# Retention products regrouped, and feed-forward steps paced anew, in a one-core retention and feed-forward kernel

## The chip, the cores and the metric

The kernel runs on one core of one Trainium2 chip. The metric is the device time of one execution in microseconds (us), lower is better. A time is a median of several executions; a ratio is the mean time of one kernel's fast runs over the mean of the other's in the same rounds, so not quite the ratio of the medians. "Faster" or "slower" is said from 2% on; smaller differences are read from the 95% intervals and from the traces. All runs quoted here are of the fast state.

Names used throughout: TensorE (PE in the profile; PEld are its weight loads), VectorE (DVE), ScalarE (ACT), GpSimd (POOL).

## The reference

```python
# retention: B=8, H=8, S=576, D=64
scores = (1/sqrt(D)) * q @ k.T
ret    = scores * Dmat            # Dmat = gamma_h ** (i - j) for i >= j, else 0
attn   = ret @ v
# bridge: (B,H,S,D) -> x of (B*S, H*D) = (4608, 512)
h   = maximum(x @ w_in, 0)        # w_in (512, 2048)
out = (h * h) @ w_out             # w_out (2048, 512)
```

## The kernel before

Retention runs in chunks of 128 tokens (the last of each batch has 64), 40 in all, with a running state `u`. The feed-forward layer runs on blocks of 512 tokens. Block 0 is done in 16 plain "steps" (4 matmuls of 128x512, which the profile counts as 8), while the weights are still being converted; every later block is 28 steps of 4 smaller matmuls (Strassen-like products). The two are interleaved on TensorE: groups of small retention products, then some steps, and so on. After the last chunk come the remaining steps and the second layer (the last 403 us of the profile), which the change does not touch.

Of a chunk the retention does: transposes of q and k (`turn`), products inside the chunk for its second half (`retain_a`), products with the state (`retain_b`), scores of the next chunk (`scores`), products inside the chunk for its first half (`retain_c`), each with 8 heads.

```python
    def retain_c(i):
        own, grow = within(i, 0)
        more = ci + 1 < NCH
        if i < N_EARLY or i >= N_CH - 2:
            # a copy of 2 elements of x: retain_c waits for retain_b through it
            nc.scalar.copy(u_sb[(2 * ci + (cs // CH)) % 3][:, 0:2, 0:1], xp[0][:, :, cs - CH:cs - CH + 1])
        ...                                    # products, 2 of x and 2 of u at a time
        if more:
            grown(i, 1)                        # state u from PSUM to SBUF, on ScalarE
        ...
            while steps and steps[0][0] <= (n - 2 if n > 4 else n - 3):
                step()                         # forced: x's room is wanted
                owed[0] -= 1
            nc.scalar.copy(xT[n]..., p...)     # x from PSUM to SBUF

    def ffn(i):                                # called three times a chunk
        if tok < TOK + R_0:
            rate = (N_W1 - 2) / R_0 if tok >= TOK else 0
        elif tok < 5 * TOK:
            rate = (3 * N_MP * NP - LAG) / (4 * TOK - TOK - R_0 + TOK)
        else:
            rate = N_MP * NP / TOK
        owed[0] += cs / 3 * rate
        while steps and owed[0] >= 1:          # may be no step at all
            owed[0] -= 1
            step()
    ...
            retain_a(i - 1);  ffn(i - 1);  convert(6)
            retain_b(i - 1)
            if i < N_CH: scores(i)
            ffn(i - 1);  convert(6)
            if i + 1 < N_CH: turn(i + 1)
            retain_c(i - 1)
            ffn(i - 1);  convert(6)
```

`convert(6)` issues the six parts in which one piece of the first layer's weights is converted: five operations on VectorE and, in their midst, a pair of activations on ScalarE; a step of block 0 needs its piece. The comments in the code are mine. The program keeps `retain_c` from running beside `retain_b`, since both add into the same PSUM from different rows of the array: a step between them does it, and where there is none, the small copy. No run here tries it without.

Of the kernel before, what the change touches and what calls it, by code (L numbers as in the profile page):

```python
# [15 lines left out]
C = 128  # L16
CH = C // 2
TOK = 512
# [22 lines left out]
def kernel(  # L41
# [33 lines left out]
    nc = tc.nc  # L75
    ctx.enter_context(tc.manual_schedule())

    B, H, S, D = q.shape
# [7 lines left out]
    N_MP = N_M // 2  # L86
    N_MQ = N_M // 2
    N_BLK = n_tok // TOK
    NP = len(PRODUCTS)
    NCH = -(-S // C)  # L90
    chunks = [(b, ci, ci * C, min(C, S - ci * C)) for b in range(B) for ci in range(NCH)]
    N_CH = len(chunks)
# [62 lines left out]
    N_W1 = N_DF  # L155
# [124 lines left out]
    def fetch_raw(count):  # L280

        for _ in range(count):
            if n_raw[0] < min(N_W1, n_made[0] + N_RAW):
                fetch_w(n_raw[0])
                n_raw[0] += 1
# [23 lines left out]
    def convert(count):  # L309
        for _ in range(count):  # L310
            f = next(w_in_steps, None)
            f and f()
# [14 lines left out]
    for half in range(2):  # L327
        at = slice(CH * half, CH * half + CH)
# [4 lines left out]
    u_sb = [only.tile([128, HP, D], F32, name=f"u_sb{j}") for j in range(3)]  # L333
# [3 lines left out]
    N_EARLY = TOK // C  # L337
# [12 lines left out]
    def rows(half, n=64):  # L350
        return slice(64 * half, 64 * half + n)
# [4 lines left out]
    xp = [None]  # L356
    clean = set()

    def clears(half, bank):

        new = (half, bank) not in clean
        clean.add((half, bank))
        return new

    def turn(i):

        cs, c0 = chunks[i][3], chunks[i][2]
        n_h = cs // CH
        p = ps_t.tile([128, 2, 512], F32, tag="t", name="t_ps").rearrange("p h (j d t) -> p h j d t", j=2, d=HP)
        for j in (1, 0):  # L370
            for hp in range(HP):
                for h in range(n_h):
                    nc.tensor.transpose(p[:, h, j, hp, :], loaded[i][j][rows(h), 2 * hp:2 * hp + 2, :],  # L373
                                        ident[rows(h), rows(h)])
        for j, name in ((1, "kT"), (0, "qT")):
            t = st[i][name] = work2.tile([128, HP, C], F32, tag=name, name=name) if j == 0 else work.tile([128, HP, C], F32, tag=name, name=name)
            to = t[:, :, :cs].rearrange("p d (h t) -> p h d t", h=n_h)
            if j:
                nc.scalar.copy(to, p[:, :n_h, j, :, :])
            else:  # L380
                nc.vector.tensor_tensor(to, p[:, :n_h, j, :, :], dq[:, :, c0:c0 + cs].rearrange("p d (h t) -> p h d t", h=n_h),
                                        op=ALU.mult)
# [31 lines left out]
    def within(i, h):  # L414

        s = st[i]
        b_, ci, c0, cs = chunks[i]
        own, grow = [], []
        for hp, e, b in HEADS:
            own.append(lambda hp=hp, e=e, b=b: nc.tensor.matmul(  # L420
                x_at(hp, b, h), lhsT=s["vs"][rows(h), 2 * hp + b, :], rhs=s["ret"][rows(h), e, hp, :],
                start=clears(b, hp // 2), stop=False, skip_group_check=True))
            grow.append(lambda hp=hp, e=e, b=b: nc.tensor.matmul(  # L423
                u_ps[0][rows(e), hp, :], lhsT=loaded[i][1][rows(1 - h), 2 * hp + e, :], rhs=s["vs"][rows(1 - h), 2 * hp + b, :],
                start=(ci == 0 and h == 1 and hp == 0), stop=(hp == HP - 1), skip_group_check=True))
        return own, grow

    def grown(i, h):
        nc.scalar.copy(u_sb[(2 * chunks[i][1] + h + 1) % 3], u_ps[0])

    def retain_a(i):

        b_, ci, c0, cs = chunks[i]
        xp[0] = ps_x.tile([128, 2, 256], F32, tag="x", name="x_ps", padded_shape=[128, 2, 512])
        clean.clear()
        if ci == 0:
            u_ps[0] = ps_u.tile([128, HP, D], F32, tag="u", name="u_ps")
        if cs < C:
            return
        own, grow = within(i, 1)  # L440
        for j in range(0, len(own), 2):
            for f in own[j:j + 2] + grow[j:j + 2]:
                f()
        grown(i, 0)

    def retain_b(i):

        s = st[i]
        b_, ci, c0, cs = chunks[i]
        for h in reversed(range(cs // CH)):  # L450
            if 2 * ci + h == 0:
                continue
            u = u_sb[(2 * ci + h) % 3]
            for hp, e, b in HEADS[0:2] + HEADS[4:6] + HEADS[2:4] + HEADS[6:8]:
                nc.tensor.matmul(x_at(hp, b, h), lhsT=u[rows(e), hp, :], rhs=s["qT"][rows(e), hp, CH * h:CH * h + CH],  # L455
                                 start=clears(b, hp // 2), stop=False, skip_group_check=True)

    def retain_c(i):

        b_, ci, c0, cs = chunks[i]  # L460
        own, grow = within(i, 0)
        more = ci + 1 < NCH
        if i < N_EARLY or i >= N_CH - 2:

            nc.scalar.copy(u_sb[(2 * ci + (cs // CH)) % 3][:, 0:2, 0:1], xp[0][:, :, cs - CH:cs - CH + 1])
        for j in range(0, len(own), 2):
            for f in own[j:j + 2] + (grow[j:j + 2] if more else []):
                f()
        if more:
            grown(i, 1)  # L470
        tok = b_ * S + c0
        at = tok
        p = xp[0][:, :, 0:256].rearrange("p a (g t) -> p a g t", g=2)
        while at < tok + cs:
            n = at // TOK

            while steps and steps[0][0] <= (n - 2 if n > 4 else n - 3):
                step()
                owed[0] -= 1
            end = min(tok + cs, (n + 1) * TOK)  # L480
            nc.scalar.copy(xT[n][:, :, at - n * TOK:end - n * TOK].rearrange("p (a g) t -> p a g t", a=2),  # L481
                           p[:, :, :, at - tok:end - tok])
            at = end
            if n_next[0] < N_BLK and (n_next[0] + 1) * TOK <= at:
                steps.extend(block_steps(n_next[0]))
                n_next[0] += 1
        st[i] = loaded[i] = None
# [137 lines left out]


    steps = []
    owed = [0.0]
    w_out_steps = w_out_parts()
    n_w2 = [0]  # L630

    def block_steps(n):
        if n == 0:
            return [(0, first_in, j) for j in range(N_W1)]
        return [(n, ffn_in, n, mp, j) for mp in range(N_MP) for j in range(NP)]

    def step():
        n, f, *args = steps.pop(0)
        f(*args)

    n_next = [0]



    R_0 = TOK * 5 // 4
    LAG = 7

    def ffn(i):

        b, ci, c0, cs = chunks[max(0, min(i, N_CH - 1))]  # L650
        tok = b * S + c0
        if tok < TOK + R_0:
            rate = (N_W1 - 2) / R_0 if tok >= TOK else 0
        elif tok < 5 * TOK:
            rate = (3 * N_MP * NP - LAG) / (4 * TOK - TOK - R_0 + TOK)
        else:
            rate = N_MP * NP / TOK
        owed[0] += cs / 3 * rate
        while steps and owed[0] >= 1:
            owed[0] -= 1  # L660
            step()

    turn(0)
    for i in range(N_CH + 1):
        if i <= N_EARLY:

            convert((0, 0, 2, 5, 5)[i])
            if i >= 1:
                retain_a(i - 1)
                retain_b(i - 1)  # L670
                retain_c(i - 1)
            convert((0, 0, 1, 1, 1)[i])
            if i == N_EARLY:
                step()
            scores(i)
            if i == N_EARLY:
                convert(6)
                step()
            turn(i + 1)
            if i == N_EARLY:  # L680
                convert(5)
        else:
            retain_a(i - 1)
            ffn(i - 1)
            convert(6)
            retain_b(i - 1)
            if i < N_CH:
                scores(i)
            ffn(i - 1)
            convert(6)  # L690
            if i + 1 < N_CH:
                turn(i + 1)
            retain_c(i - 1)
            ffn(i - 1)
            convert(6)
        if i + 3 < N_CH:
            load(i + 3)
        if i < N_EARLY:
            fetch_raw(1)
# [210 lines left out]
```

## Time and profile before

| | before |
|---|---|
| time, median of 4 runs | 1025.22 us (1019.52 to 1026.13) |
| profiled execution | span 1019.0 us |
| TensorE busy | 983.6 us (97%) |
| VectorE, ScalarE, GpSimd busy | 751.6, 184.9, 80.3 us |

TensorE is the bound; its 35.4 us of idle time and the time lost inside "busy" are all there is to win. The lines that carry this are in the prediction. One table more tells who TensorE waited for (us in total, times, longest; the seven largest rows of its matmuls). It is the table to compare with every later run:

```profile
PE t_ps L373 <- DVE ret L406: 7.8, 5, 5.4
PE t_ps L373 <- DMA k_ld<-in_k_dram: 5.9, 6, 3.2
PE x_ps L455 <- ACT u_sb L429: 3.0, 6, 0.6
PE sc_ps L399 <- DVE qT L381: 2.8, 2, 1.8
PE o_a L790 <- DMA a<-g_dram: 2.6, 1, 2.6
PE x_ps L420 <- ACT room L481: 1.9, 1, 1.9
PE x_ps L420 <- ACT u_sb L465: 1.8, 5, 0.7
```

The transposes (`t_ps`) waited 7.8 us for the masking of the scores (`ret`), because both share one PSUM tile. The last row is the small copy, which only six chunks have here. The profiled execution was among the fastest of this kernel (1020.7 us), so differences of times are read from the timed runs and the trace is used to say where they lie.

### The profile page before, as it was taken

The page shows a single profiled execution, that of the slowest core. Times are in us where ns is not written, and L with a number is a line of the kernel's source. Part 1 is how long each engine was busy: PE and PEld are TensorE (multiplying, and loading weights), DVE is VectorE, ACT ScalarE, POOL GpSimd, SP SyncE. Part 2 cuts the span into 40 slices and gives each one's busy share as a digit, 9 for nine tenths or more (in the row PEclk, how much of TensorE's full clock was granted, in tenths as well). Part 3 has the DMA queues.
Part 4 walks back from the last instruction along what each step waited for, and adds up shares of the span by engine and source line. Part 5 has one row for each costly group of instructions (what it writes and reads, how often), then busy time and mean ns, then how long its engine had stood idle before and what let it go on. Part 6 is the DMA issues. An engine that isn't in the chain of part 4 may idle for free.

```text
span 1019.0 us, 24086 instructions
## 1 busy us (share of the span) xinstructions
PE 983.6 (97%) x10376; PEld 862.1 (85%) x10376; DVE 751.6 (74%) x1418; ACT 184.9 (18%) x425; POOL 80.3 (8%) x82
## 2 busy tenths in 40 slices
PE   6789999999999999999999998999999999999998
PEld 4444488888888788888788888999999999999997
DVE  2679577666888887888886776877777677777765
ACT  2435221111312213212221000000000000000000
POOL 1100001101111011110101000000000000000000
PEclk9789999999999999999999999999999999999999
DMA  8965547737578669669537898784855747565351
GB/s 201 236 191 162 131 154 204 195 122 208 159 241 270 188 227 268 219 211 288 178 146 271 337 420 307 279 288 157 290 201 200 271 167 258 193 232 207 124 207 42
DMA packets 187658, 220.34 MB, mean 216 GB/s; under 512 B 119200, under 2 KB 137632, under 8 KB 178592
## 3 DMA queue, kind: packets, MB, share of 16 engines
q1 hardware_dynamic: 187552, 218.81, 65.8%
q8 instruction: 81, 1.33, 0.5%
q14 instruction: 25, 0.20, 0.1%
HBM read 129.39 MB, written 89.39 MB: 215 GB/s over the span
## 4 chain that ended last, share of the span: by engine, by line
PE 90%; DVE 4%; DMA 2%; SPq 2%; issue 1%; ACT 1%; DVEq 0%; ACTq 0%
PE h_b L578 17%; PE o_b L790 16%; PE h_c L578 11%; PE h_a L578 11%; PE o_c L790 11%; PE o_a L790 11%; PE h_ps L543 5%; PE x_ps L420 3%; PE t_ps L373 2%; PE x_ps L455 2%; PE sc_ps L399 1%; DMA a<-g_dram 1%; DMA k_ld<-in_k_dram 1%; PE u_ps L423 1%; SPq L142 1%
## 5 line engine op out<-in xcount | busy, mean ns | idle before, releaser
L578 PE MATMUL h_b<-room,w 128*128 128x256 f32 x736 | 178.0, 385 | 0.0
L578 PEld LDWEIGHTS h_b<-room,w 128*128 128x128 f32 x736 | 136.5, 190 | 19.9 <-DVE room L597 0.3
L790 PE MATMUL o_b<-w,room 128*128 128x128 f32 x1168 | 144.5, 275 | 0.2 <-DVE room L741 0.2
L790 PEld LDWEIGHTS o_b<-w,room 128*128 128x128 f32 x1168 | 137.2, 192 | 0.5 <-DVE room L741 0.4
L790 PE MATMUL o_c<-w,room 128*128 128x128 f32 x1008 | 123.0, 275 | 0.0
L790 PEld LDWEIGHTS o_c<-w,room 128*128 128x128 f32 x1008 | 117.7, 192 | 0.0
L578 PE MATMUL h_c<-room,w 128*128 128x256 f32 x480 | 115.9, 384 | 0.0
L578 PE MATMUL h_a<-room,w 128*128 128x256 f32 x448 | 106.9, 381 | 0.0
L578 PEld LDWEIGHTS h_c<-room,w 128*128 128x128 f32 x480 | 89.2, 190 | 12.8
L578 PEld LDWEIGHTS h_a<-room,w 128*128 128x128 f32 x448 | 84.3, 190 | 12.2 <-issue 0.5
L790 PE MATMUL o_a<-w,a 128*128 128x128 f32 x688 | 85.9, 275 | 2.6 <-DMA a<-g_dram 2.6
L790 PEld LDWEIGHTS o_a<-w,a 128*128 128x128 f32 x688 | 81.3, 192 | 2.9 <-issue 2.8
L585 DVE SCALAR_TENSOR_TENSOR room<-room 128x512 f32<-128x512 f32 x96 | 69.7, 726 | 3.3
L595 POOL TENSOR_TENSOR room<-room 128x512 f32<-128x512 f32 x32 | 35.9, 1121 | 441.8 <-ACT room L594 358.7
L801 ACT COPY r<-o_a 128x128 f32<-128x128 f32 x54 | 14.4, 266 | 276.9 <-PE o_a L790 246.3
L543 PE MATMUL h_ps<-room,w 128*128 128x512 f32 x128 | 62.7, 636 | 1.0 <-ACT room L481 1.0
L420 PEld LDWEIGHTS x_ps<-ret,v_ld 64*64 64x64 f32 x1152 | 42.4, 143 | 20.1 <-issue 13.6
L597 DVE TENSOR_TENSOR room<-h_b,room 128x512 f32<-128x512 f32 x32 | 22.1, 691 | 50.1 <-PE h_b L578 47.7
L420 PE MATMUL x_ps<-ret,v_ld 64*64 64x64 f32 x1152 | 52.6, 234 | 5.7 <-ACT room L481 1.9
L408 POOL TENSOR_TENSOR v_ld<-v_ld,dv 128x512 f32<-128x512 f32 (+1 forms) x40 | 44.2, 1108 | 90.3 <-DMA v_ld<-in_v_dram 69.7
L543 PEld LDWEIGHTS h_ps<-room,w 128*128 128x128 f32 x128 | 24.5, 201 | 28.0 <-issue 25.7
L588 ACT COPY room<-h_a 128x512 f32<-128x512 f32 x32 | 18.8, 587 | 157.4 <-PE h_a L578 157.4
(94 smaller groups left out, 1361.1 us busy)
## 6 DMA issues: line engine op xcount, KB each, us to landing
g_dram<-room SPq DMA_DIRECT2D x32, 1792.0 KB, 7.3
a<-g_dram SPq DMA_DIRECT2D x43, 1024.0 KB, 6.8
room<-g_dram SPq DMA_DIRECT2D x20, 1024.0 KB, 6.0
w<-w_dram SPq DMA_DIRECT2D x7, 1792.0 KB, 12.2
out_dram<-room SPq DMA_DIRECT2D x18, 512.0 KB, 3.3
v_ld<-in_v_dram SPq DMA_DIRECT2D x32, 256.0 KB, 3.8
w<-in_moe_w_in_dram SPq DMA_DIRECT2D x16, 512.0 KB, 5.0
w<-in_moe_w_out_dram SPq DMA_DIRECT2D x16, 512.0 KB, 3.8
```

Of the source, the lines that this page charges most:

```text
L373: nc.tensor.transpose(p[:, h, j, hp, :], loaded[i][j][rows(h), 2 * hp:2 * hp + 2, :], ident[rows(h), rows(h)])
L408: nc.gpsimd.tensor_tensor(vs[:cs], vs[:cs], dv[:cs, :, ci:ci + 1].to_broadcast([cs, H, D]), op=ALU.mult)
L420: own.append(lambda hp=hp, e=e, b=b: nc.tensor.matmul(x_at(hp, b, h), lhsT=s["vs"][rows(h), 2 * hp + b, :], rhs=s["ret"][rows(h), e, hp, : ...
L455: nc.tensor.matmul(x_at(hp, b, h), lhsT=u[rows(e), hp, :], rhs=s["qT"][rows(e), hp, CH * h:CH * h + CH], start=clears(b, hp // 2), stop=Fa ...
L543: nc.tensor.matmul(p.rearrange("p h t -> p (h t)"), lhsT=w[:, c, :], rhs=xT[0][:, c, :], start=(c == 0), stop=(c == N_DM - 1))
L578: nc.tensor.matmul(p[:, mm, :], lhsT=w[:, c, :], rhs=xs[n][right][:, c, :], start=(j in OPENS and mm == 0 and c == 0), stop=(j in CLOSES a ...
L585: nc.vector.scalar_tensor_tensor(t, t, 0.0, t, op0=ALU.max, op1=ALU.mult)
L588: nc.scalar.copy(p1, p)
L595: nc.gpsimd.tensor_tensor(g["A11"], g["A11"], g["A11"], op=ALU.mult)
L597: nc.vector.tensor_tensor(g["A22"], p, p15, op=ALU.add)
L790: nc.tensor.matmul(p, lhsT=s["lefts"][left][:, m, :], rhs=w_out[j][:, m, WO_SLOT[right], :], start=(i in OPENS and m == 0), stop=(i in CLO ...
L801: nc.scalar.copy(r[:, 0, 0:128], p)
```

## The change

Its intent is fewer goings to and fro between retention and steps (two groups per chunk, not three), at least one step between any two groups, and a line that says how many steps should be done at which token. Core of the diff, comments added, cuts marked:

```diff
     def retain_b(i):
         ...
+        # now in every chunk, at the end of the products with the state
+        nc.scalar.copy(u_sb[(2 * ci + (cs // CH)) % 3][:, 0:2, 0:1], xp[0][:, :, cs - CH:cs - CH + 1])
     def retain_c(i):
-        if i < N_EARLY or i >= N_CH - 2:
-            nc.scalar.copy(...)               # the same copy
         ...
-        if more:
-            grown(i, 1)
         ...
             nc.scalar.copy(xT[n]..., p...)
+            if more and at == tok:
+                grown(i, 1)                   # behind x's copy
-    def ffn(i): ...                           # rates, as above
+    PACE = ((4 * TOK + HALF // 4, N_W1 + 2 * N_MP * NP - 2), ...)
+    def ffn(i, half):                         # called twice a chunk
+        gone[0] += chunks[...][3] / 2
+        if steps and steps[0][0] == 0:        # block 0: a step and its conversion together
+            step(); convert(6)
+            if half and steps and steps[0][0] == 0:
+                step(); convert(6)
+            return
+        ...                                   # want = the line through PACE at this token
+        if steps:
+            step()                            # never none while steps are left
+        while steps and done[0] < int(want):
+            step()
...
-            retain_a(i - 1);  ffn(i - 1);  convert(6)
-            retain_b(i - 1)
-            if i < N_CH: scores(i)
-            ffn(i - 1);  convert(6)
-            if i + 1 < N_CH: turn(i + 1)
-            retain_c(i - 1)
-            ffn(i - 1);  convert(6)
+            retain_a(i - 1)
+            if i < N_CH: turn(i)
+            ffn(i - 1, 0)
+            retain_b(i - 1)
+            if i < N_CH: scores(i)
+            retain_c(i - 1)
+            ffn(i - 1, 1)
```

More of the change, by code (lines that the diff above doesn't have):

```diff
@@ L462, in retain_c @@
         more = ci + 1 < NCH
-        if i < N_EARLY or i >= N_CH - 2:
-            nc.scalar.copy(u_sb[(2 * ci + (cs // CH)) % 3][:, 0:2, 0:1], xp[0][:, :, cs - CH:cs - CH + 1])
         for j in range(0, len(own), 2):
@@ L478, in retain_c @@
                 step()
-                owed[0] -= 1
             end = min(tok + cs, (n + 1) * TOK)
@@ L627 @@
     steps = []
-    owed = [0.0]
     w_out_steps = w_out_parts()
@@ L638, in step @@
         n, f, *args = steps.pop(0)
+        done[0] += 1
         f(*args)
     n_next = [0]
-    R_0 = TOK * 5 // 4
-    LAG = 7
-    def ffn(i):
-        b, ci, c0, cs = chunks[max(0, min(i, N_CH - 1))]
-        tok = b * S + c0
-        if tok < TOK + R_0:
-            rate = (N_W1 - 2) / R_0 if tok >= TOK else 0
-        elif tok < 5 * TOK:
-            rate = (3 * N_MP * NP - LAG) / (4 * TOK - TOK - R_0 + TOK)
-        else:
-            rate = N_MP * NP / TOK
-        owed[0] += cs / 3 * rate
-        while steps and owed[0] >= 1:
-            owed[0] -= 1
+    HALF = C // 2
+    PACE = ((4 * TOK + HALF // 4, N_W1 + 2 * N_MP * NP - 2), (5 * TOK - HALF, N_W1 + 3 * N_MP * NP - 2),
+            (6 * TOK + HALF // 4, N_W1 + 4 * N_MP * NP - 2), (8 * TOK + HALF // 4, N_W1 + 6 * N_MP * NP - 2),
+            (9 * TOK, N_W1 + 7 * N_MP * NP - 2))
+    done = [0]
+    gone = [0]
+    behind = []
+    def ffn(i, half):
+        gone[0] += chunks[max(0, min(i, N_CH - 1))][3] / 2
+        if steps and steps[0][0] == 0:
+            step()
+            convert(6)
+            if half and steps and steps[0][0] == 0:
+                step()
+                convert(6)
+            return
+        if not behind:
+            behind.append((gone[0] - HALF, done[0]))
+        points = behind + [p for p in PACE if p[0] > behind[0][0]]
+        want = points[-1][1]
+        for (x0, y0), (x1, y1) in zip(points, points[1:]):
+            if gone[0] < x1:
+                want = y0 + (y1 - y0) * (gone[0] - x0) / (x1 - x0)
+                break
+        if steps:
+            step()
+        while steps and done[0] < int(want):
             step()
@@ L678 @@
                 step()
-            turn(i + 1)
-            if i == N_EARLY:
+            if i < N_EARLY:
+                turn(i + 1)
+            else:
                 convert(5)
         else:
+            if i == N_EARLY + 1:
+                gone[0] = TOK
             retain_a(i - 1)
-            ffn(i - 1)
-            convert(6)
+            if i < N_CH:
+                turn(i)
+            ffn(i - 1, 0)
             retain_b(i - 1)
@@ L688 @@
                 scores(i)
-            ffn(i - 1)
-            convert(6)
-            if i + 1 < N_CH:
-                turn(i + 1)
             retain_c(i - 1)
-            ffn(i - 1)
-            convert(6)
+            ffn(i - 1, 1)
         if i + 3 < N_CH:
```

## The prediction

> **What bounds the kernel now.** I read the page's busy shares first, then its slices, then the costliest groups, then TensorE's idle times along the timeline.
>
> ```profile
> PE 983.6 (97%) x10376; PEld 862.1 (85%) x10376; DVE 751.6 (74%) x1418; ACT 184.9 (18%) x425; POOL 80.3 (8%) x82
> PE   6789999999999999999999998999999999999998
> PEclk9789999999999999999999999999999999999999
> ```
>
> TensorE is the bound: 983.6 of 1019.0 us busy, and the chain of waits gives it 90% of the span. What it multiplies is the same in both kernels. So the change can win only three things: TensorE's idle time (35.4 us in all), time at a low clock (the 7 in PEclk, slice two), and time hidden inside "busy", where matmuls are far apart. About 10.7 us of the idle time lies before 30 us, 2.9 at 600 to 640 us (a transfer of the second layer's input) and 5.0 at the end; the change touches none of these. What it can touch lies between 42 and 545 us:
>
> ```profile
> 48.82 0.69 PE L399 MATMUL sc_ps<-qT,kT 64*64 64x64 f32 x32 [1.01 <-DVE qT L381]
> 54.87 0.69 PE L373 MATMUL t_ps<-ident,k_ld 64*128 64x64 f32 x8 [5.36 <-DVE ret L406]
> 56.96 5.72 PE L543 MATMUL h_ps<-room,w 128*128 128x512 f32 x8
> ...
> 88.64 0.27 PE L420 MATMUL x_ps<-ret,v_ld 64*64 64x64 f32 x2 [1.85 <-ACT room L481]
> ```
>
> Two groups of retention stand here with no feed-forward step between them; the second group's transposes wait 5.36 us for VectorE, which is converting weights. Behind that wait one step (8 instructions) takes 5.72 us, against 3.70 elsewhere. From 42 to 545 us I count twelve such waits: 1.01, 5.36, 1.85, 0.36, 0.82, 0.57, 0.80, 0.55, 0.44, 1.42, 0.50, 0.74, together 14.4 us.
>
> The hidden time shows in one whole chunk, from 209.22 to 224.89 us. It holds three groups of retention products with two or three steps between:
>
> ```profile
> 209.22 1.99 PE L578 MATMUL h_b<-room,w 128*128 128x256 f32 x8
> 211.06 1.89 PE L578 MATMUL h_c<-room,w 128*128 128x256 f32 x8
> 212.88 0.27 PE L420 MATMUL x_ps<-ret,v_ld 64*64 64x64 f32 x2
> ...
> 213.50 1.99 PE L578 MATMUL h_a<-w,w 128*128 128x256 f32 x8
> 215.33 1.89 PE L578 MATMUL h_b<-w,w 128*128 128x256 f32 x8
> 217.15 0.69 PE L455 MATMUL x_ps<-qT,u_sb 64*64 64x64 f32 x32
> 217.67 0.65 PE L399 MATMUL sc_ps<-qT,kT 64*64 64x64 f32 x32
> 218.24 1.99 PE L578 MATMUL h_c<-w,w 128*128 128x256 f32 x8
> 220.07 1.89 PE L578 MATMUL h_b<-room,w 128*128 128x256 f32 x8
> 221.80 1.89 PE L578 MATMUL h_a<-w,w 128*128 128x256 f32 x8
> 223.62 0.46 PE L373 MATMUL t_ps<-ident,k_ld 64*128 64x64 f32 x8
> ```
>
> Read the starts, not the durations. Inside a burst one step follows the other after 1.73 us (220.07 to 221.80); next to a group it takes 1.82 or 1.83. The chunk lasts 15.67 us. Seven steps at 1.73 are 12.11. The products themselves: transposes 0.65, two sets of 8 pairs at 0.06 (0.48 each), products with the state 0.52, scores 0.46, together 2.59. What remains, 15.67 - 12.11 - 2.59 = 0.97, belongs to three goings in and out of a group: 0.32 us each.
>
> **What the Trainium skill says.** "TensorEngine Tiling (Array Packing)", Key Properties, says that changing the tiling mode drains TensorE. Retention uses tiles of 64 rows, the steps 128; the 0.32 us agree with it. "TensorE: Matmul & The Clock Gate", Why this matters for your kernels, warns that an idle gap over about 3 us drops the clock. The trace agrees: after the 5.36 us gap the granted clock from 57 to 63.3 us is 0.68. The same page's table at the top calls ScalarE's queue strictly first in, first out, 8 deep; this matters below, and the trace's order of ScalarE's instructions fits it.
>
> **The change part by part.**
>
> 1. Three groups become two: the transposes go behind the first group, the last group behind the scores. In the order of the two built programs I count entries from a step into retention: 95 before, 72 after, so 23 fewer. (A chunk of 64 tokens has no first group and saves nothing.) 23 x 0.32 = 7.4 us, all on TensorE's path.
>
> 2. At least one step between any two groups, and steps spread along a line instead of the bursts of six that x's room forced. Of the 14.4 us of waits I expect 13.7 to go; the last one, 0.74 at 543.50, stays, since there are no more scores behind which to hide it. The lines above show bunched groups for the largest of them. The low clock goes too: the step costs 62.6 - 56.96 = 5.65 instead of 3.63 (2.0), the groups before it about 1.0 more than elsewhere. Together 16.7 us.
>
> 3. A wait is added. The last retention products write the same PSUM as those with the state but from other rows of the array; a step between used to keep them apart. Now a small ScalarE copy reads that PSUM in every chunk, and the last products wait for it. Before, only the first chunks and the last two had it, fully exposed:
>
> ```profile
> 20.24 1.14 PE L455 MATMUL x_ps<-qT,u_sb 64*64 64x64 f32 x32 [0.50 <-ACT u_sb L429]
> 21.45 0.16 ACT L465 COPY u_sb<-x_ps 128x2 f32<-128x2 f32 x1 [1.25 <-PE x_ps L455]
> 21.66 0.37 PE L420 MATMUL x_ps<-ret,v_ld 64*64 64x64 f32 x2 [0.28 <-ACT u_sb L465]
> ```
>
> The copy starts 0.07 us after the products end, takes 0.16, and TensorE goes on 0.05 later. At full clock the products end 0.69 us after their start (217.15), so the last group may begin at 0.97. TensorE itself, with 32 scores in between, gets there at 0.52 + 0.46 = 0.98. If ScalarE is free the wait is just hidden; with the 16 scores of a half chunk TensorE is there at about 0.77 and waits 0.2.
>
> ScalarE isn't always free. In block 0, in four chunks, its order is: eviction of the step just ended (0.60), two activations of the weight conversion (0.72 and 0.66), then this copy. From the step's end that is about 2.2 us against 0.9 (0.65 with half the state products): 1.3 twice and 1.55 twice, 5.7 us. Later, five chunks have the two activations directly ahead of the copy; where they come from the very last step I expect 1.2 us, otherwise nothing, so about 3 us. An eviction alone costs 0.1 in some ten chunks, 1.0. Seven half chunks at 0.2 make 1.4. Sum: 11 us given back.
>
> 4. Transposes to scores: two thirds of a chunk's steps before, half now, in two places one step of 1.8 us. The path from transposes to scaled q is two evictions in a row (0.59 and 0.69 us) plus what VectorE has queued. I put 1.0 us on it, and 0.5 on block 1's first operand sums.
>
> 5. The state copy moves behind x's copy (0.59 us later); its reader comes one half chunk of steps later, so nothing.
>
> Sum: 7.4 + 16.7 - 11 - 1.5 = 11.6 us shorter.
>
> **The rivals.**
>
> The added wait eats the gain. It is in every chunk; if ScalarE were late by 0.7 us in all 36, that is 25 us, and the time would stay at 1020 to 1026. For it: a strict queue, and conversion activations that themselves wait for VectorE (24.7 us of such waits in the list). Against it: ScalarE is 18% busy, 12.17 of 50 us between 350 and 400 us, and most chunks have only one eviction ahead of the copy, often from an earlier step.
>
> VectorE becomes the bound. Between 400 and 450 us it is busy 43.6 of 50 us; 2% less time makes that 89%. Three banks for three accumulations leave it about one step before TensorE has to wait. For it: bursts of four steps are more frequent now. Against it: the old program had bursts of four and six with no wait of TensorE's in the steps, and the unbroken steps from 550 to 600 us run at 50.00 of 50. It would make 1016 to 1020.
>
> The wait list is fully won and the copy costs nothing: 7.4 + 16.7 = 24 us, 1000. For it: nothing but the sums above without their third item. Against it: the four chunks of block 0, where the order on ScalarE is plain.
>
> Feared but excluded: the second layer (382 us) shifts as a whole. Its first transfers are issued at the same steps of the last block, where the old kernel waits 2.65 us for one; I expect that again.
>
> **Range and chances.** The three timed runs are 1019.52, 1025.22 and 1026.13; the profiled one 1020.7. From a typical 1023.5 us less 11.6 I get 1012. The uncertain items are the 11 us (5 to 18) and the 16.7 (12 to 17), and the spread of 6 us between the runs: 1003 to 1019. Faster by over 2% needs below 1004.7, which takes nearly the third rival: 0.13. Slower by over 2% would take a stall I have not seen: 0.02. Within 2%: 0.85.
>
> **What would show each step right or wrong.** (1) A chunk's two groups with 0.32 us per entry; the sum of time between steps, with bursts at 1.73 us. (2) No wait for the score mask's result near 50 us, PEclk 9 there soon after 45 us, no 5.7 us step behind. (3) A new row in TensorE's waits: the last products waiting for the small copy, 1 to 1.6 us each in block 0, at most a few tenths mostly after. (4) Scores waiting for scaled q, where one step stands between. I am wrong if those waits for the copy add up to over 18 us or under 5, if steps wait for VectorE's evictions, or if the second layer's start waits longer than 3 us.

## The result, and the profile after

1009.18 us (median of 4 runs, 1006.41 to 1012.22) against 1025.22: ratio 0.9856, 95% interval 0.981 to 0.9901. That is within 2%, though clearly below 1. The forecast was 1012 us in a range of 1003 to 1019.

The page's first lines of the changed kernel:

```profile
span 1004.7 us, 24101 instructions
PE 975.3 (97%) x10376; PEld 862.4 (86%) x10376; DVE 749.7 (75%) x1418; ACT 188.9 (19%) x459; POOL 81.8 (8%) x82
PEclk9999999999999999999999999999999999999999
```

The same instructions on TensorE take 8.3 us less of busy time, and idle time falls from 35.4 to 1004.7 - 975.3 = 29.4 us. PEclk no longer drops in slice two. ScalarE has 34 instructions more: the small copies.

Who TensorE waited for, in the changed kernel (the small copy is now on line 458):

```profile
PE x_ps L420 <- ACT u_sb L458: 9.1, 13, 1.4
PE t_ps L373 <- DMA k_ld<-in_k_dram: 4.4, 4, 3.2
PE o_a L800 <- DMA a<-g_dram: 2.7, 1, 2.7
PE sc_ps L399 <- DVE qT L381: 2.0, 1, 2.0
PE x_ps L455 <- ACT u_sb L429: 2.0, 4, 0.5
PE h_b L576 <- DVE room L504: 1.2, 1, 1.2
```

The row of the transposes waiting for `ret` is gone, and the copy heads the list with 9.1 us, 7.3 more than before. One new wait of a step stands below: 1.2 us for the sums of a block's first operand.

A whole chunk with seven steps, on TensorE's timeline (start, duration, what). Compare it with the one in the prediction:

```profile
209.13 1.99 PE L576 MATMUL h_a<-w,w 128*128 128x256 f32 x8
...
216.23 0.69 PE L455 MATMUL x_ps<-qT,u_sb 64*64 64x64 f32 x32
216.75 0.65 PE L399 MATMUL sc_ps<-qT,kT 64*64 64x64 f32 x32
217.21 0.27 PE L420 MATMUL x_ps<-ret,v_ld 64*64 64x64 f32 x2
...
217.83 1.99 PE L576 MATMUL h_b<-w,w 128*128 128x256 f32 x8
...
223.84 0.46 PE L373 MATMUL t_ps<-ident,k_ld 64*128 64x64 f32 x8
224.13 0.42 PE L373 MATMUL t_ps<-ident,q_ld 64*128 64x64 f32 x8
224.48 2.00 PE L576 MATMUL h_a<-w,w 128*128 128x256 f32 x8
```

From 209.13 to 224.48 it lasts 15.35 us, where the old one took 15.67: 0.32 us less, the price put on one entry. Inside a burst the steps still follow each other by 1.73 us; what went is one going in and out of a group.

The second layer shifts as a whole: its first product starts at 616.42 us before and at 602.08 after, 14.34 us earlier, and from there to the end it takes 402.6 us in both. So all that the trace gained lies ahead of it.

What the copy waits for in block 0, on ScalarE's timeline, with TensorE's line behind it:

```profile
50.42 0.60 ACT L545 ACTIVATE room<-h_ps 128x512 f32<-128x512 f32 x1 [3.08 <-PE h_ps L541]
50.92 0.71 ACT L213 ACTIVATE w<-w,exp_bias 128x512 uint32<-128x512 uint32 x1
51.53 0.65 ACT L214 ACTIVATE w<-w 128x512 f32<-128x512 uint32 x1
52.07 0.15 ACT L458 COPY u_sb<-x_ps 128x2 f32<-128x2 f32 x1
```

```profile
50.61 0.69 PE L399 MATMUL sc_ps<-qT,kT 64*64 64x64 f32 x32
52.37 0.68 PE L420 MATMUL x_ps<-ret,v_ld 64*64 64x64 f32 x16 [1.06 <-ACT u_sb L458]
```

The queue stands in the order foreseen: eviction, two activations of the conversion, copy. TensorE stood idle for 1.06 us. The other three chunks of block 0 lost 1.03, 0.81 and 0.81.

### The profile page after: what moved, and what is told of

The parts are those of the page before. It is cut to its first block, busy times and chain, and to the rows that moved or that the text cites. A ratio compares the mean times of both kernels' runs of the same rounds, so it can differ in the third digit from the quotient of the medians.

```text
span 1004.7 us, 24101 instructions
## 1 busy us (share of the span) xinstructions
PE 975.3 (97%) x10376; PEld 862.4 (86%) x10376; DVE 749.7 (75%) x1418; ACT 188.9 (19%) x459; POOL 81.8 (8%) x82
## 4 chain that ended last, share of the span: by engine, by line
PE 87%; DVE 7%; DMA 2%; ACT 2%; SPq 2%; issue 1%; DVEq 0%
PE o_b L800 16%; PE h_b L576 15%; PE o_c L800 11%; PE o_a L800 11%; PE h_a L576 10%; PE h_c L576 9%; PE h_ps L541 6%; PE x_ps L420 3%; PE t_ps L373 2%; PE x_ps L455 2%; DMA a<-g_dram 1%; PE sc_ps L399 1%; DVE room L583 1%; SPq L142 1%; DMA k_ld<-in_k_dram 1%
## 5 line engine op out<-in xcount | busy, mean ns | idle before, releaser
L583 DVE SCALAR_TENSOR_TENSOR room<-room 128x512 f32<-128x512 f32 x96 | 67.4, 702 | 3.3
L541 PE MATMUL h_ps<-room,w 128*128 128x512 f32 x128 | 59.9, 616 | 0.8 <-ACT room L477 0.7
L807 DVE TENSOR_TENSOR small<-o_b,small 128x128 f32<-128x128 f32 x63 | 18.3, 291 | 38.5 <-PE o_b L800 38.4
```

The source lines that it names most:

```text
L541: nc.tensor.matmul(p.rearrange("p h t -> p (h t)"), lhsT=w[:, c, :], rhs=xT[0][:, c, :], start=(c == 0), stop=(c == N_DM - 1))
L583: nc.vector.scalar_tensor_tensor(t, t, 0.0, t, op0=ALU.max, op1=ALU.mult)
L807: nc.vector.tensor_tensor(s["u2"], p, s["p1"], op=ALU.add)
```

## The experiments

Eleven runs in three sittings (the number e8 was not used); each sitting ran the kernel before beside them. All gave correct results.

| run | what | median us | ratio to before | 95% interval |
|---|---|---|---|---|
| changed kernel | | 1009.18 | 0.9856 | 0.981 to 0.9901 |
| e1 | new pacing, three groups | 1016.94 | 0.9917 | 0.9894 to 0.9939 |
| e2 | two groups, old pacing | 1031.62 | 1.0063 | 1.0037 to 1.0089 |
| e3 | changed, one group split | 1013.88 | 0.9897 | 0.9878 to 0.9915 |
| e4 | before, one step moved | 1018.65 | 0.9938 | 0.9923 to 0.9954 |
| after_again | changed kernel, repeated | 1008.86 | 0.9846 | 0.9818 to 0.9874 |
| e5 | changed, longer copy | 1017.18 | 0.9922 | 0.9896 to 0.9947 |
| e6 | changed, block 0's conversion behind the copy | 1005.21 | 0.9819 | 0.9792 to 0.9846 |
| e7 | as e6, and the later conversion too | 1000.63 | 0.9768 | 0.974 to 0.9795 |
| e9 | changed, old rates in place of the line | 1007.16 | 0.9841 | 0.9823 to 0.9859 |
| e10 | before, block 0's new rule alone | 1011.67 | 0.9875 | 0.9854 to 0.9896 |
| e11 | e7 repeated | 1000.59 | 0.9774 | 0.9755 to 0.9792 |

The theory was that of the prediction: entries into retention cost 0.32 us each, a step between groups takes away waits, the small copy gives part of it back. Rivals: only the grouping counts, or only the pacing; and of the copy, that it costs nothing, or that it is slow everywhere.

### e1: the new pacing with three groups

Condensed from the diff:

```diff
-            retain_a(i - 1); turn(i); ffn(i - 1, 0)
-            retain_b(i - 1); scores(i); retain_c(i - 1); ffn(i - 1, 1)
+            retain_a(i - 1); ffn(i - 1, 0)
+            retain_b(i - 1); scores(i); ffn(i - 1, 0)
+            turn(i + 1); retain_c(i - 1); ffn(i - 1, 1)      # thirds; the copy only where it was before
```

> The new line of steps with the old three groups, so without the added copy wait in the middle chunks. Theory (a group entry costs 0.32 us, pacing and the entries are separate gains): 102 entries against 72 in the changed kernel, 30 x 0.32 = 9.6 us more, less 6.2 us of copy waits after 42 us: 3.4 us slower than the changed kernel, ratio to the kernel before 0.989. Rival, the grouping is worth nothing: the copy waits alone go, ratio 0.980. Rival, pacing is worth nothing: 1.000 or a little over.

Measured 0.9917, near the 0.989 of the theory and away from both rivals. It is slower than expected by about 3 us, and the trace names a wait that I had not counted:

```profile
PE h_b L576 <- DVE room L504: 5.9, 5, 1.7
PE t_ps L373 <- DMA k_ld<-in_k_dram: 5.4, 5, 3.3
PE t_ps L373 <- DVE ret L406: 3.5, 6, 1.3
```

The first row: steps that wait for the sums of a block's first operand, five times; the changed kernel has one such wait. So the agreement is partly luck: these waits (4.7 us more) and the third row (3.5) are about what the copy's waits gave back (9.1 to 1.1 us). TensorE's idle time is the same in both profiles (29.2 and 29.4 us); what differs is its busy time, 985.8 against 975.3 us. Of these 10.5 us, 1.7 are a spell of half clock (granted clock 0.50 for about 3.4 us) in the second layer; the 8.8 left are 0.29 us for each of the 30 entries.

### e2: two groups with the old pacing

The changed kernel with the old rates, called twice a chunk, and conversion in nines, since there are two places for it and not three. So it differs from both kernels in how conversion is lumped.

> Two groups with the old rates and forced bursts; conversion of 9 parts at each of two places instead of 6 at three. Theory: 68 entries, 27 x 0.32 = 8.6 us gained on the kernel before, copy waits 6 us lost, waits between groups with no step (x for its copy, state copy, scores for q) back at 8 to 12 us of the old 14.4: ratio 0.992 to 0.997. Rival, pacing is worth nothing: same as the changed kernel, 0.986.

Measured 1.0063: outside what either side expected, and slower than the kernel before although TensorE enters retention 27 times less. Its waits:

```profile
PE x_ps L420 <- ACT u_sb L458: 14.0, 13, 2.2
PE sc_ps L399 <- DVE qT L381: 10.4, 4, 3.5
```

The scores now wait for the scaled q, since no step stands between the transposes and them; and the copy waits longer, since more conversion is ahead of it in ScalarE's queue. What I had left out is what such gaps do to the clock. Windows of this run: start and end, length, then busy time by engine (x instructions), granted clock, DMA share and GB/s:

```profile
51.50:58.20 6.70, 5.75 (x39) 3.00 (x30) 6.56 (x13) 1.56 (x4) 0.00 (x0) 0.50 0.98 263
85.60:89.00 3.40, 3.40 (x20) 1.59 (x11) 3.37 (x7) 0.86 (x2) 0.15 (x1) 0.50 0.58 132
89.10:95.00 5.90, 5.90 (x60) 2.99 (x59) 4.24 (x7) 2.50 (x5) 2.13 (x2) 1.00 0.52 136
```

Behind the gap of 3.51 us that ended at 51.05 the clock is halved, 0.50, for 6.7 us. Behind gaps of 2.19, 1.96, 1.95 and 1.95 us (ended at 67.70, 85.11, 102.46 and 156.59) it is 0.50 for about 3.4 us and then 1.00 again, which is 1.7 us of full clock each. So a gap can cost more than its length, and grouping without pacing made just such gaps here; how much of that is due to the conversion in nines, no run tells.

### e3: one group split

```diff
             retain_a(i - 1)
             if i < N_CH:
+                if chunks[i - 1][3] == C and len(steps) > 1 and steps[0][0] > 0:
+                    step()
                 turn(i)
```

> The changed kernel with one of its steps put between the first group's products and the transposes: 24 more group entries, nothing else. Theory: 24 x 0.32 = 7.7 us slower than the changed kernel, ratio 0.993. Rival, the entry costs nothing by itself: 0.986.

Measured 0.9897, so 0.0041 to 0.0051 above the changed kernel's two results: 4 to 5 us, not 7.7. The profiled run is 7.6 us longer, but part of that is another thing: two spells of half clock of 1.7 us each, which the changed kernel's profile lacks. One, from 306 to 310 us, stands behind a wait of 1.86 us for the first operand's sums, where the changed kernel waits 1.21 us and keeps 1.00; the other, at 627 us, is in the second layer. TensorE's busy time is 7.5 us longer (982.8 us); without the two spells 4.1 us, 0.17 for each of the 24 entries. The chunk itself tells the price of the split:

```profile
209.87 1.99 PE L576 MATMUL h_a<-w,w 128*128 128x256 f32 x8
211.80 0.46 PE L373 MATMUL t_ps<-ident,k_ld 64*128 64x64 f32 x8
...
225.42 0.92 PE L576 MATMUL h_a<-w,w 128*128 128x256 f32 x3
```

Seven steps again, 15.55 us from 209.87 to 225.42, against 15.35: 0.20 us for this entry, and 24 x 0.20 = 4.8 us, within the 4 to 5 timed. Why 0.20 and not 0.32: products and transposes don't have the same tiling (64x64 and 64x128), so their junction isn't free either; in the changed kernel the transposes begin 0.17 us after the last pair of products (208.31 and 208.48), where pairs follow each other by 0.06. That this 0.11 is the difference fits, but no run took it apart further. The last group behind the scores, which is what the change joined, has the same tiling on both sides and saves the full 0.32.

### e4: the kernel before with one step moved

```diff
             ffn(i - 1)
             convert(6)
+            if i == N_EARLY + 1:
+                step()
             if i + 1 < N_CH:
                 turn(i + 1)
```

> The kernel before with one single step of block 0 moved ahead of the transposes that waited 5.36 us. Theory: that wait and the low clock behind it go, 5.36 + 3.0 = 8.4 us, ratio 0.992, PEclk 9 or more in slice two. Rival, only the wait goes and the clock stays low: 5.4 us, 0.995. Rival, the wait for VectorE's conversion reappears a few us later: 1.000.

Measured 0.9938, 6.4 us. The wait shrank from 5.36 to 1.72 us (one step of 3.7 us covers just so much), 3.64 us, and the clock behind it stayed up:

```profile
56.40 0.46 PE L373 MATMUL t_ps<-ident,k_ld 64*128 64x64 f32 x8 [1.72 <-DVE ret L406]
...
57.65 3.70 PE L543 MATMUL h_ps<-room,w 128*128 128x512 f32 x8
```

The step behind it takes 3.70 us, not 5.72. In the window from 57 to 63.3 us the granted clock is 1.00 (0.68 before). 3.64 + 3.0 for the clock makes 6.6: the prediction's size for the clock holds, and the 3.64 alone lies outside the interval (4.7 to 7.9 us). Expected was 8.4, since I had thought that the whole wait would go. (The two profiled spans, 1017.2 and 1019.0 us, differ by less: this execution has two spells of half clock, at 87 and 633 us, that the other lacks, 3.4 us together, and its second step starts 1.5 us later, at 44.60 against 43.07.)

### after_again

> The changed kernel once more, to stand beside the next three on the same chip. Ratio to the kernel before 0.982 to 0.989; if it is near 0.983, the third group of the run before cost its 7 us in time and not only in the trace.

0.9846; the changed kernel's ratio repeats.

### e5: a longer copy

```diff
-        nc.scalar.copy(u_sb[...][:, 0:2, 0:1], xp[0][:, :, cs - CH:cs - CH + 1])
+        nc.scalar.copy(u_sb[...].rearrange("p (a g) d -> p a g d", a=2),
+                       xp[0][:, :, 0:256].rearrange("p a (g t) -> p a g t", g=2)[:, :, :, cs - CH:cs])
```

> The changed kernel with a longer small copy: 256 elements of each partition in place of 2, 0.37 us in place of 0.16. Theory (the copy is only just hidden behind the scores, 0.97 against 0.98 us): nearly each of some 35 chunks waits 0.2 us longer, 6 to 7 us more than the changed kernel, and the count of waits for it rises from 13 to over 30. Rival, there is slack and only the chunks with a full ScalarE queue wait: 13 x 0.2 = 2.7 us, count 13 to 16.

Measured 0.9922, 7.8 us over the changed kernel in the same sitting. First the changed kernel's row for the weight loads (its row for the matmuls, 9.1 us in 13 waits, stands above), then both rows of this run:

```profile
PEld x_ps L420 <- ACT u_sb L458: 7.9, 10, 1.6
```

```profile
PEld x_ps L420 <- ACT u_sb L458: 13.9, 32, 1.8
PE x_ps L420 <- ACT u_sb L458: 12.2, 14, 1.6
```

The matmul row counts few waits more, since a matmul's modelled end covers a short gap; the weight loads show it, 32 waits against 10. So the copy of 0.16 us is hidden with next to nothing to spare, in most of the 40 chunks. In the two profiles of this sitting the span is 10.6 us longer (1018.1 against 1007.5): 3.0 in the matmul row (12.2 against 9.2), 7.8 inside TensorE's "busy" (984.0 against 976.2). Of the latter, 3.4 are two spells of half clock that the other profile lacks, at 412 us behind a wait of 1.54 us for this copy and at 635 us in the second layer.

### e6 and e7: conversion behind the copy

e6 puts block 0's conversion behind the copy; e7 also the two activations of the later conversion (the second layer's weights, a part with each later step), where they come from the last step ahead of the copy.

```diff
             retain_b(i - 1)                  # ends with the copy
+            while held:                      # e7
+                held.pop(0)()
+            convert(behind_copy[0])          # e6; what fills held is cut
+            behind_copy[0] = 0
             if i < N_CH:
                 scores(i)
...
         if steps and steps[0][0] == 0:
             step()
+            if not half:
+                behind_copy[0] = 6
+                return
             convert(6)
```

> The changed kernel with block 0's conversion, which stood between the step and the small copy in ScalarE's queue, put behind the copy. Theory: the four waits of 0.8 to 1.06 us in block 0 (3.7 us) go, ratio 0.003 to 0.004 below the changed kernel's. Rival, the conversion being later makes VectorE late and a step or the scores wait: no gain.

> As the one before, and also the later conversion's two activations are put behind the copy where they come from the last step ahead of it. Theory: waits of 1.32 and 0.82 us go too, 5 to 6 us in all below the changed kernel, waits for the copy under 2 us. Rival as before.

e6 measured 0.9819, 0.0027 below the changed kernel in the same sitting; the intervals overlap, so the time alone doesn't settle it. Its waits for the copy fell from 9.2 us (13) to 5.4 (9), as expected. e7 measured 0.9768, 8 us below the changed kernel in the same sitting where 5 to 6 were expected, and leaves 1.5 us (5) of such waits. ScalarE at the same place as above:

```profile
51.25 0.60 ACT L547 ACTIVATE room<-h_ps 128x512 f32<-128x512 f32 x1 [3.23 <-PE h_ps L543]
51.74 0.16 ACT L460 COPY u_sb<-x_ps 128x2 f32<-128x2 f32 x1
51.78 0.74 ACT L213 ACTIVATE w<-w,exp_bias 128x512 uint32<-128x512 uint32 x1
```

The copy is done at 51.90, right behind the eviction. This takes the activations from ahead of the copy (VectorE's part of block 0's conversion moves behind it with them), and 7.6 us of the 9.1 go, about what the time gained: the wait was ScalarE's strict order, as "TensorE: Matmul & The Clock Gate" has it in the table at its top.

### e9: old rates in place of the line

```diff
-        want = ...                           # the line through PACE
-        while steps and done[0] < int(want):
-            step()
+        owed[0] += cs / 2 * rate             # the old rates; at least one step as before
+        while steps and owed[0] >= 1:
+            owed[0] -= 1
+            step()
```

> The changed kernel with block 0's rule (a step and its conversion together) and the step between any two groups kept, but the line of steps replaced by the old rates. Theory: the step between groups is what the pacing brings, not the line; 72 entries as in the changed kernel, forced bursts remain but none joins two groups: ratio within 0.003 of the changed kernel's 0.985. Rival, the line itself carries the gain: 0.990 or more.

Measured 0.9841, not to be told from the changed kernel's 0.9846 and 0.9856. The line itself brings nothing that the times show. What pacing brings must lie in the two things kept, a step between any two groups and block 0's rule; e10 takes the second alone.

### e10: block 0's rule alone

```diff
     def ffn(i):
+        if steps and steps[0][0] == 0:
+            step()
+            convert(6)
+            return
         ...
-            ffn(i - 1); convert(6)           # three times
+            ffn(i - 1)
```

> The kernel before with block 0's new rule alone, three groups and old rates otherwise. Theory: most of the pacing's gain (8.5 us with the whole of it) lies in block 0, the 5.36 us wait and what follows it; 101 entries against 95 cost 1.9 us: ratio 0.991 to 0.993. Rival, the later waits carry it: 0.997.

Measured 0.9875, 12.8 us: more than expected, and more than the whole pacing with three groups (e1), which pays its first-operand waits. Of its transposes' waits for `ret` only two are left:

```profile
PE t_ps L373 <- DVE ret L406: 2.0, 2, 1.9
```

Where it came from is told by TensorE's busy time (the number behind the length of the stretch; the clock is the third from the end) in the stretch of block 0 and in a later one, first before, then e10:

```profile
36.00:130.00 94.00, 82.84 (x901) 43.42 (x898) 64.55 (x107) 36.06 (x70) 8.22 (x7) 0.92 0.64 171
300.00:553.00 253.00, 248.54 (x2985) 207.40 (x2985) 208.87 (x352) 60.60 (x121) 34.92 (x32) 1.00 0.72 225
```

```profile
36.00:130.00 94.00, 90.49 (x1032) 49.74 (x1025) 69.95 (x117) 37.97 (x74) 7.91 (x9) 0.98 0.73 200
300.00:553.00 253.00, 251.36 (x2998) 210.00 (x2997) 208.01 (x352) 61.27 (x121) 34.56 (x33) 1.00 0.71 226
```

Idle time in block 0's stretch fell from 11.2 to 3.5 us and the clock rose from 0.92 to 0.98; later it fell from 4.5 to 1.6 us. (Part of the 0.92 cost nothing: the clock was also at about half from 36 to 41 us (mean 0.54), yet the step there took 5.41 us, and 5.42 at full clock in the changed kernel.) The later part I had not expected: the old rates begin their count behind block 0 here, and in the order of the built program the bursts of six steps are gone. So most of the gain is in block 0, a smaller part in the later stretch, where the bursts are the likely cause, and none of it needs the regrouping. From here to e9, which adds the two groups and the copy, 0.0034 are left, 3.5 us, though the intervals just overlap: 101 entries become 72, 9.3 us at 0.32 each, of which the copy's waits (6.1 against 2.0 us) and some others take back over half.

### e11

> The fastest version so far once more, to see that its ratio of 0.977 to the kernel before repeats: 0.974 to 0.980.

0.9774: e7's result repeats. It is the fastest kernel of this study, 2.3% below the kernel before.

## Why the prediction was right

The sum was 7.4 + 16.7 - 11 - 1.5 = 11.6 us; measured are 14.8 us (1025.22 x 0.0144) and 15.8 us in the repetition.

1. *Three groups become two, 7.4 us.* Right. The chunk became shorter by 0.32 us, as worked out. That the change of tiling mode is what costs it rests on the page that the prediction names; the runs show the size, and that it depends on the groups joined. e3 shows that the price of an entry depends on what is joined: 0.20 between products and transposes, which have different tilings.

2. *A step between groups, 13.7 us of waits and 3.0 us of low clock.* Right in mechanism, nearly in size. None of the listed waits but the last is left (0.37 us), and PEclk is up. e4 shows the clock's share by itself. e10 gets 12.8 us from block 0's rule and what follows from it, and it has six entries more than the kernel before (101 against 95, an estimated 1.9 us from 0.32 each). The runs put nothing on the line of steps, which the prediction had credited (e9).

3. *The copy gives 11 us back.* The mechanism was right, ScalarE's queue in four chunks of block 0 and a few later ones; this term was mis-sized and is why the forecast was too slow. It measured 7.3 us (9.1 less the 1.8 that were there before). In block 0 I had 1.3 to 1.55 us per chunk, measured were 0.81 to 1.06: 3.7 us for four chunks, not 5.7. My 2.2 us chained the durations, but each instruction of the queue starts about 0.1 us before the one ahead ends (50.42 + 0.60 = 51.02, next start 50.92), so that TensorE went on 1.96 to 2.05 us after the step's end. As much of the error or more was TensorE's own way there: it was at the copy 0.93 to 1.16 us after the step, not 0.65 to 0.9. The later conversion cost 3.9 us in four waits (1.42, 1.32, 0.82, 0.33), where I had about 3; of the 2.4 us for evictions and half chunks the matmul row shows nothing. That the copy is only just hidden elsewhere (0.97 against 0.98) is what e5 shows.

4. *New waits for scaled q and first operand, 1.5 us.* The size is right, the split not: 1.2 us for the operand's sums and 0.5 for an eviction, and after 36 us none for q.

5. *The state copy, nothing.* Nearly: x's copy now goes first, and the first step of block 0 waits 0.68 us for it, not 1.04.

With 7.3 for the third term the sum is 15.3 us, between the two measured. The rivals: that the copy eats the gain was wrong, though in e2, with more conversion ahead of it, its waits are 14.0 us. That VectorE becomes the bound was wrong too: 749.7 us busy and one eviction wait of 0.5 us. That the copy costs nothing, 1000 us, was wrong for this change and right for e7, which takes most of the copy's waits away and measures 1000.6. The second layer shifted as expected and waits 2.71 us for its transfer; the prediction's 382 us for it was TensorE's busy time in a shorter window, the layer takes 403.

What stays open: why gaps of one length halve the clock in some executions and not in others (below), and how much of the spread between runs comes from that. A spell is worth 1.7 us, so it can move a trace by more than some of the differences discussed here. It is not all of the spread: of the kernel before, one run in e1's sitting took 1021.26 us at a mean clock of 0.989 and another 1025.91 at 0.991.

## What to carry to other kernels

Before regrouping work for the sake of fewer goings in and out of a group, put a price on one change from the starts in the timeline (0.32 us here), and look for gaps of the bounding engine first: here one gap of 5.36 us, with the 3.0 us of low clock behind it, cost more than the 23 entries saved (7.4 us). A synchronising copy on another engine comes as late as what stands ahead of it in that engine's queue (e6, e7): issue it ahead of work that can wait. When conversion and consumption run together, issue them in step, one piece with one use, rather than at separate rates.

## What the Trainium skill lacked or had wrong

- "TensorE: Matmul & The Clock Gate", Why this matters for your kernels, warns of idle gaps over about 3 us. Shorter ones can do it: after gaps of 1.95 to 2.19 us (e2), 1.86 (e3), 1.85 (e4, at 87.31 us) and 1.54 (e5) the clock was halved for about 3.4 us. Not always: after 1.85 us in the kernel before (at 88.64 us, the same place in the program) it was 1.00, after 1.72 us in e4 1.00. The wait for the second layer's transfer, 2.58 to 3.05 us, stands in all 13 profiles: the clock was halved behind it in seven (2.58 us among them) and not in six (3.05 us among them), so the length does not decide it.
- "TensorEngine Tiling (Array Packing)", Key Properties, says that a mode change drains TensorE and gives no time. Here, if that is the cause, going from 128-row steps into a group of 64-row products and back costs 0.32 us, and 0.20 where the split parts a 64x64 from a 64x128 group.
- I found no page that gives the time for TensorE to wait on a small copy of its own PSUM by ScalarE. Here the copy starts 0.07 us after the products' modelled end, takes 0.16 and TensorE goes on 0.05 later (kernel before, at 21.45 us, with ScalarE free).
